# Row 0 of a fused attention and expert kernel: dilated transposes moved forward, dilated v cast by its load, the last product stored in two parts

## The chip, the cores and the metric

The kernel runs on one core of a Trainium2 chip. The metric is the device time of one execution in microseconds (us). Of the kernel before, five runs and one profiled execution are shown.

## What is computed

Attention over 8 batch rows, each with 8 heads, 576 positions and 64 numbers per head, then an expert layer over all 4608 tokens. Heads 0 to 3 look at the last 32 positions ("sliding"), heads 4 to 7 at every fourth of the last 128 ("dilated").

```
scores = q @ k.T / sqrt(64);  masked outside the window
attn   = exp(scores - max) / (sum + 1e-9)
x      = (attn @ v), heads side by side: 4608 x 512
out    = relu(x @ w_in)**2 @ w_out        # w_in 512 x 2048, w_out 2048 x 512, out float32
```

## The kernel before

The program is unrolled and written in order by hand: each engine carries out its instructions in the order in which the source issues them, and the framework adds the waits. What orders the work around the change is therefore the source order and the queues: SyncE's (SP) and GpSimd's (POOL) each issue their transfers one after the other, and a transfer that waits holds up those behind it.

Tokens go through the expert layer in nine chunks of 512 columns (`mm1_gen`: products with w_in, line 298, relu on ScalarE, line 321, square on VectorE, line 322; then products with w_out). Chunks 2 to 8 take the second product by one level of Strassen's scheme (`mm2_strassen_gen`): seven products of halves, in PSUM banks called a, b and c (matmuls in line 375), joined by copies on ScalarE (line 391) and sums on VectorE (line 402) in the SBUF tiles `ou` and `ov`, and stored by `leave` (line 397). Attention of row b is written between steps ("pump") of the expert chunk before it, so TensorE has expert matmuls while other engines do softmax.

Row 0 has no chunk before it. There TensorE is kept occupied by `fill_gen` (line 507): pairs of 128x512 matmuls whose result nobody reads, one pair for each pump. Row 0 goes as follows.

- GpSimd issues four loads that cast float32 to float16: `ns` (sliding k, then q, line 112) and `nd` (dilated k, then q, line 103). GpSimd then makes a position table and the identity matrix.
- VectorE clears tiles and makes the masks `maskp` and `maskd`. It writes into `sv` and `sd` a few values of `ns` (lines 759, 761), which holds back SyncE's loads of v into those tiles until `ns` is there.
- SyncE loads v in float32 into the staging tiles `sv` (six loads, line 129) and `sd` (two loads, line 137). GpSimd casts them into `vp` (line 169) and `vd` (line 177), with a fourth column block for the row sums; between these casts it issues the three parts of w_in (`wi`, line 146).
- TensorE transposes q and k (`t_sliding`, line 536; `t_dilated`, line 553); VectorE and ScalarE copy the results to `QKTp` and `QKTd` (lines 163, 165).
- Scores (`s_sliding`, line 573, twice; `s_dilated`, line 592, twice) go to PSUM tiles of a pool with two buffers; ScalarE takes the exponential (line 563), VectorE multiplies by the mask (line 564).
- ScalarE copies the overlap of neighbouring blocks inside `vp` and `vd` ("halo", lines 184, 189).
- Values (`av_sliding`, line 622, three times; `av_dilated`, line 638, four times) are divided by the row sums on VectorE (reciprocal, line 605, product, line 610), transposed on TensorE (lines 651, 669) and copied into `xT` on ScalarE (lines 657, 675). Then the first expert chunk starts.

The order of row 0 in the source before:

```
t_sliding x2; s_sliding 0; fill; s_sliding 1; fill; halo; t_dilated x2; halo; fill;
av_sliding 0; fill; s_dilated 0; fill; s_dilated 1; fill; halos; av_sliding 1 and 2; ...
```

The tile `sd` also serves later rows; its upper 64 partitions of the first part are cleared once at the start. The pool `gp`, with two buffers, holds the hidden values `g` of the expert chunks. [...]

Of the kernel before, what the change touches and what calls it, by code (L numbers as in the profile page):

```python
# [8 lines left out]
FP16 = mybir.dt.float16  # L9
# [4 lines left out]
P = 128  # L14
# [3 lines left out]
def kernel(  # L18
# [9 lines left out]
    nc = tc.nc  # L28

    B, H, S, D = q.shape  # L30
    W = 32
    DIL = 4
# [3 lines left out]
    HH = H // 2  # L36
# [62 lines left out]
    def load_qk(b):  # L99
        n = load_sliding_qk(b)  # L100
        m = natp.tile([P, 36 * D], FP16, name=f"nd{b}", tag="n")
        for i, s in ((1, k), (0, q)):
            nc.gpsimd.dma_start(
                out=m[64 * i : 64 * (i + 1), :],
                in_=s[b, HH:H].rearrange("h (p j) d -> (h p) (j d)", j=36),
            )
        return n, m
# [23 lines left out]
            for h in (0, 2):  # L131
                nc.sync.dma_start(out=sv[PADP:P, h : h + 2], in_=vv[:, h : h + 2])

    def load_dilated_v(b, eng):
        vv = v[b, HH:H].rearrange("h (i c) d -> i h (c d)", c=DIL)
        for t in range(2):
            eng.dma_start(out=sd[P - QD[t] : P, t, :, :], in_=vv[Q0D[t] : Q0D[t] + QD[t]])
# [2 lines left out]
        load_sliding_v(b)  # L140
        load_dilated_v(b, nc.sync)

    def load_w_in():
        f0 = 0
        for t, w in zip(wi, wi_cols):
            nc.gpsimd.dma_start(
                out=t, in_=moe_w_in[:, f0 : f0 + w].rearrange("(dh dl) f -> dl dh f", dl=P)
            )
            f0 += w

    def load_w_out(gs):
        for g in gs:
# [14 lines left out]
    def cast_sliding_v(b, ms=range(0, NB, 2)):  # L167
        for m in ms:
            nc.gpsimd.tensor_copy(  # L169
                vp[b % 2][:, m : m + 2, :, 0:D], sv[:, :, m : m + 2, :].rearrange("p h m d -> p m h d")  # L170
            )

    def cast_dilated_v(b):
        for t in range(2):
            p0 = 64 * t
            for c in range(0, DIL, 2):
                nc.gpsimd.tensor_copy(  # L177
                    vd[b % 2][p0:P, t, c : c + 2, :, 0:D],
                    sd[p0:P, t, :, D * c : D * (c + 2)].rearrange("p h (c d) -> p c h d", d=D),
                )  # L180

    def halo_sliding(b, mp):
        m0, m1 = max(1, 2 * mp), 2 * mp + 2
        nc.scalar.copy(
            vp[b % 2][0:PADP, m0:m1, :, 0:D], vp[b % 2][P - PADP : P, m0 - 1 : m1 - 1, :, 0:D]
        )
# [49 lines left out]


    nsd = {0: load_qk(0)}
    warm = const.tile([P, 1], FP32, name="warm")
    nc.vector.memset(warm, 0.0)  # L240
    nc.scalar.activation(warm, warm, ACTF.Exp)
    nc.vector.memset(sv[0:PADP, :, 0, :], 0.0)
    nc.vector.memset(sd[0:64, 0, :, :], 0.0)
    nc.vector.memset(sv[0:PADP, :, 1:NB, :], 0.0)
    for r in range(2):
        nc.vector.memset(QKTp[r][:, 1, :, 0:PADP], 0.0)
# [5 lines left out]
    reli = const.tile([P, QB], I16, name="reli")  # L252
    nc.gpsimd.iota(reli, pattern=[[1, QB]], base=0, channel_multiplier=-1)
    make_identity(nc, ident)

    relf = const.tile([P, QB], FP32, name="relf")
    nc.vector.tensor_copy(relf, reli)
# [95 lines left out]
    def mm2_strassen_gen(c, g):  # L353
        A, Bk, Ck = "abc"
        banks = {}

        def wq(r, q):
            return lambda k: wo[2 * r + k // 4][:, k % 4, HM * q : HM * (q + 1)]

        def gq(i, r):  # L360
            return lambda k, t: g[:, HF * r + k, HTOK * i + P * t : HTOK * i + P * (t + 1)]

        def tq(n):
            return lambda k: wt[n][:, k]

        def sq(n):
            return lambda k, t: gs[n][:, k, P * t : P * (t + 1)]

        def product(bank, a, b, ts=(0, 1)):
            new = bank not in banks  # L370
            if new:
                banks[bank] = pmool.tile([P, 2, HM], FP32, name=f"p{bank}{c}", tag="pm")
            for t in ts:
                for k in range(HF):
                    nc.tensor.matmul(  # L375
                        banks[bank][:, t],
                        a(k, t),
                        b(k),
                        start=(new and t == 0 and k == 0),
                        stop=(k == HF - 1),  # L380
                        skip_group_check=True,
                    )
                    if k % 4 == 3 and (t, k) != (ts[-1], HF - 1):
                        yield

        def half(i):
            return otp.tile([P, 2, DM], FP32, name=f"o{i}_{c}", tag="ot")

        def take(o, j):
            ot = o[:, :, HM * j : HM * (j + 1)]  # L390
            nc.scalar.copy(ot, banks[A])  # L391
            return ot

        def leave(o, i, js):
            t0 = c * TOKC + HTOK * i
            m = slice(HM * js[0], HM * (js[-1] + 1))
            nc.sync.dma_start(
                out=out[t0 : t0 + HTOK, m].rearrange("(t p) m -> p t m", p=P), in_=o[:, :, m]
            )

        def add(ot, bank):
            nc.vector.tensor_add(ot, banks[bank], ot)  # L402

        last = c == NTOKC - 1

        nc.vector.tensor_sub(g[:, 0:HF, HTOK:], g[:, 0:HF, 0:HTOK], g[:, 0:HF, HTOK:])
        yield from product(A, gq(0, 0), wq(0, 0))
        upper = half("u")
        o11 = take(upper, 0)
        yield  # L410
        yield from product(Ck, gq(0, 1), wq(1, 0), (0,))
        yield
        yield from product(A, sq(1), tq(1))
        lower = half("v")
        o21 = take(lower, 0)
        yield
        yield from product(Bk, gq(1, 0), tq(2))
        nc.vector.tensor_sub(gs[1], g[:, HF:, 0:HTOK], gs[1])
        yield
        yield from product(A, sq(0), tq(0))  # L420
        o22 = take(lower, 1)
        add(o22, Bk)
        if last:
            leave(lower, 1, (1,))
        yield
        yield from product(Ck, gq(0, 1), wq(1, 0), (1,))
        add(o11, Ck)
        if last:
            leave(upper, 0, (0,))
        yield  # L430
        yield from product(A, sq(1), wq(1, 1))
        take(upper, 1)
        leave(upper, 0, (1,) if last else (0, 1))
        yield
        yield from product(Bk, gq(1, 1), tq(3))
        add(o21, Bk)
        leave(lower, 1, (0,) if last else (0, 1))
        yield

    def mm2(c, g, po, t, ffc):  # L440
# [71 lines left out]
    def pump(n):  # L512
        for _ in range(n):
            while pending:
                try:
                    next(pending[0])
                    break
                except StopIteration:
                    pending.pop(0)
# [28 lines left out]
    def t_dilated(b, n, a, wide):  # L548
        for w, (s0, s1) in enumerate(((0, 5), (5, 9))):
            p_ = pt(f"pd{b}_{a}_{w}", wide)  # L550
            for s in range(s0, s1):
                j = 4 * s + 2 * a
                nc.tensor.transpose(  # L553
                    p_[:, P * (s - s0) : P * (s - s0 + 1)], n[:, D * j : D * (j + 2)], ident
                )
            copy(
                nc.scalar if w else nc.vector,
                QKTd[b % 2][:, :, a, KPAD:].rearrange("x i (c s) -> x i c s", s=9)[:, :, :, s0:s1],
                p_[:, 0 : P * (s1 - s0)].rearrange("x (s i c) -> x i c s", i=2, c=64),
            )  # L560
# [5 lines left out]
    def s_sliding(b, hp):  # L566
        tiles = [pa(f"ps{b}_{hp}_{half}") for half in range(2)]
        for half, ps in enumerate(tiles):
            for m3 in range(3):
                m = 3 * half + m3  # L570
                for e in range(2):
                    r = slice(D * e, D * (e + 1))
                    nc.tensor.matmul(  # L573
                        ps[:, e, QB * m3 : QB * (m3 + 1)],
                        QKTp[b % 2][r, 1, hp, QB * m : QB * m + P],
                        QKTp[b % 2][r, 0, hp, PADP + QB * m : PADP + QB * (m + 1)],
                        start=True,
                        stop=True,
                    )
        for half, ps in enumerate(tiles):  # L580
            softmax(2 * hp + half, ps, maskp)
# [176 lines left out]
    n, m = nsd[0]  # L758
    nc.vector.tensor_copy(sv[64:P, 0, :, 0], n[0:64, 0, 0:NB])
    load_sliding_v(0)  # L760
    nc.vector.tensor_copy(sd[64:P, :, 0, 0], n[0:64, 0, 0:2])
    load_dilated_v(0, nc.sync)
    cast_sliding_v(0, (0, 2))
    load_w_in()
    cast_sliding_v(0, (4,))
    cast_dilated_v(0)
    for hp in range(2):
        t_sliding(0, n, hp, False)
    pending.append(fill_gen())
    for hp in range(2):  # L770
        s_sliding(0, hp)
        pump(1)
    halo_sliding(0, 0)
    for a in range(2):
        t_dilated(0, m, a, False)
    halo_sliding(0, 1)
    pump(1)
    xs = x_tiles(0)
    av_sliding(0, 0, xs)
    pump(1)  # L780
    for g in range(2):
        s_dilated(0, g)
        pump(1)
    halo_sliding(0, 2)
    for c in (0, 2):
        halo_dilated(0, c)
# [146 lines left out]
```

## Time and profile before

| | us |
|---|---|
| median of 5 runs (lowest, highest) | 309.16 (307.81, 311.26) |
| profiled execution, its own time | 310.32 |
| its span | 308.5 |
| TensorE busy (share) | 288.2 (93%) |
| VectorE busy | 209.6 (68%) |
| ScalarE busy | 173.2 (56%) |
| GpSimd busy | 63.9 (21%) |
| first transposes of row 0 that have k and q, start | 6.87 |
| first run of back-to-back expert matmuls, start | 26.03 |
| last sum, start | 304.68 |
| last store, issue | 305.40 |

The span is what the profiler saw between first and last instruction; the execution's own time is 1.8 us longer. A line of the timeline has start, length, engine, source line, operation, tiles and shapes, how many instructions were merged into it, and in brackets the idle time before it with what ended that. PE is TensorE, DVE VectorE, ACT ScalarE, POOL GpSimd, SP SyncE; a q behind an engine's name is its queue. Lines of the chain have start, length, engine, tile and line.

### The profile page before, as it was taken

Reading aid. Unit: us, or ns where it says so; the run is one execution under the profiler, and the core shown is the slowest. Engines: PE = TensorE matmul, PEld = TensorE weight load, DVE = VectorE, ACT = ScalarE, POOL = GpSimd, SP = SyncE. Lnnn points to the kernel's source line nnn. Section 1 sums busy time; section 2 is a strip of 40 time slices with the busy share of each in tenths; the row PEclk is TensorE's granted clock in tenths of the full one; section 3 lists DMA queues with packets and bytes.
Section 4 is the critical chain, followed back from the end, with each engine's and each line's share of the span. In section 5 each row is a group of like instructions: output and inputs, shape, how many; then the busy total and the mean of one; then the engine's idle time right before and its main releaser. Section 6 shows DMA issues by size and latency. Waiting matters only on the chain.

```text
span 308.5 us, 6899 instructions
## 1 busy us (share of the span) xinstructions
PE 288.2 (93%) x2762; PEld 193.7 (63%) x2762; DVE 209.6 (68%) x434; ACT 173.2 (56%) x293; POOL 63.9 (21%) x112
## 2 busy tenths in 40 slices
PE   1988998999999899999997999899989999999994
PEld 1544554555554468756886997458745875685584
DVE  7785447758942698489758993889388934834652
ACT  2765648668745863495356634854495436525620
POOL 4480027002803602410026002700230000000000
PEclk9999999999999999999999999999999999999999
DMA  7899999699599999995799979989891141003004
GB/s 121 190 208 211 208 158 155 150 201 234 121 214 149 253 186 187 249 205 119 124 180 265 192 128 185 277 177 140 159 255 39 23 103 52 2 1 136 2 1 137
DMA packets 77616, 47.03 MB, mean 152 GB/s; under 512 B 58480, under 2 KB 69232, under 8 KB 77584
## 3 DMA queue, kind: packets, MB, share of 16 engines
q1 hardware_dynamic: 68832, 32.96, 51.0%
q0 software_dynamic: 8752, 13.63, 25.6%
q8 instruction: 21, 0.34, 0.5%
q14 instruction: 11, 0.09, 0.1%
HBM read 36.70 MB, written 16.52 MB: 172 GB/s over the span
## 4 chain that ended last, share of the span: by engine, by line
PE 81%; DMA 9%; DVE 4%; ACT 3%; issue 1%; SPq 0%; POOL 0%; DVEq 0%; POOLq 0%
PE ph L298 33%; PE pa L375 16%; PE po L441 9%; PE pb L375 8%; DMA vp<-vp 6%; PE pc L375 4%; PE paw L638 3%; PE pav L622 2%; DMA QKTp<-dp 2%; PE ps L573 2%; DMA ns<-in_q_dram 2%; ACT AT L563 2%; PE pf L507 2%; DVE AT L564 1%; PE pd L553 1%
## 5 line engine op out<-in xcount | busy, mean ns | idle before, releaser
L298 PE MATMUL ph<-xT,wi 128*128 128x512 f16 (+1 forms) x640 | 134.2, 359 | 0.7 <-ACT xT L675 0.7
L321 ACT ACTIVATE rt<-ph 128x512 f16<-128x512 f32 x144 | 86.2, 609 | 48.4 <-PE ph L298 46.2
L298 PEld LDWEIGHTS <-wi 128*128 128x128 f16 x640 | 68.2, 114 | 45.9 <-issue 0.6
L322 DVE TENSOR_TENSOR g<-rt 128x512 f16<-128x512 f16 x144 | 62.5, 444 | 40.1 <-ACT rt L321 38.7
L375 PEld LDWEIGHTS <-g 128*128 128x128 f16 x448 | 43.3, 98 | 6.1
L375 PEld LDWEIGHTS <-gs 128*128 128x128 f16 x336 | 32.1, 98 | 3.9 <-DVE gs L332 0.3
L441 PE MATMUL po<-wo,g 128*128 128x512 f16 x128 | 33.1, 379 | 0.0
L402 DVE TENSOR_TENSOR ov<-pb,ov 128x512 f32<-128x512 f32 x14 | 9.7, 692 | 30.9 <-PE pb L375 17.4
L375 PE MATMUL pa<-wt,gs 128*128 128x256 f16 x224 | 27.2, 273 | 0.0
L375 PE MATMUL pb<-wt,g 128*128 128x256 f16 x224 | 27.1, 273 | 0.0
L169 POOL CAST vp<-sv 128x512 f16<-128x512 f32 x24 | 15.4, 671 | 55.7 <-DMA sv<-in_v_dram 51.7
L391 ACT COPY ov<-pa 128x512 f32<-128x512 f32 x14 | 8.2, 585 | 30.7 <-PE pa L375 30.7
L177 POOL CAST vd<-sd 128x512 f16<-128x512 f32 (+1 forms) x32 | 21.9, 712 | 10.7 <-PE ph L298 7.9
L610 DVE TENSOR_TENSOR xd<-paw,rcp_d 80x512 f16<-80x512 f32 (+1 forms) x32 | 21.9, 685 | 1.1
L563 ACT ACTIVATE AT<-pz 128x576 f16<-128x576 f32 x32 | 19.7, 696 | 1.5 <-PE pz L592 1.4
L563 ACT ACTIVATE AT<-ps 128x576 f16<-128x576 f32 x32 | 19.2, 658 | 2.5 <-PE ps L573 2.0
L564 DVE TENSOR_TENSOR AT<-AT,maskp 128x576 f16<-128x576 f16 x32 | 15.6, 496 | 6.3 <-ACT AT L563 4.6
L564 DVE TENSOR_TENSOR AT<-AT,maskd 128x576 f16<-128x576 f16 x32 | 18.5, 604 | 1.8 <-ACT AT L563 0.6
L391 ACT COPY ou<-pa 128x512 f32<-128x512 f32 x14 | 8.2, 586 | 16.3 <-PE pa L375 16.3
L610 DVE TENSOR_TENSOR xs<-pav,rcp_p 96x512 f16<-96x512 f32 x24 | 16.5, 686 | 0.8
L622 PEld LDWEIGHTS <-AT 128*128 128x128 f16 x192 | 9.5, 99 | 11.9 <-issue 7.3
L622 PE MATMUL pav<-vp,AT 128*128 128x65 f16 x192 | 10.9, 196 | 5.6 <-DMA vp<-vp 4.5
(80 smaller groups left out, 279.3 us busy)
## 6 DMA issues: line engine op xcount, KB each, us to landing
sv<-in_v_dram SPq DMA_DIRECT2D x14, 288.0 KB, 5.3
dp<-nr SPq DMA_DIRECT2D x12, 288.0 KB, 4.1
out_dram<-ou SPq DMA_DIRECT2D x6, 512.0 KB, 4.2
out_dram<-ov SPq DMA_DIRECT2D x6, 512.0 KB, 4.6
sd<-in_v_dram SPq DMA_DIRECT2D x8, 320.0 KB, 6.4
ns<-in_k_dram POOLq DMA_DIRECT2D x8, 288.0 KB, 6.2
ns<-in_q_dram POOLq DMA_DIRECT2D x8, 288.0 KB, 7.9
sd<-in_v_dram SPq DMA_DIRECT2D x8, 256.0 KB, 6.2
```

What stands on the lines that cost most here:

```text
L169: nc.gpsimd.tensor_copy(vp[b % 2][:, m : m + 2, :, 0:D], sv[:, :, m : m + 2, :].rearrange("p h m d -> p m h d"))
L177: nc.gpsimd.tensor_copy(vd[b % 2][p0:P, t, c : c + 2, :, 0:D], sd[p0:P, t, :, D * c : D * (c + 2)].rearrange("p h (c d) -> p c h d", d=D),)
L298: nc.tensor.matmul(ph[:, t0:t1], wi4[ffc // 4][:, dmk, :, ffc % 4], xT[:, dmk, x0 : x0 + t1 - t0], start=(dmk == 0 and t0 == 0), stop=(dmk ...
L321: nc.scalar.activation(rt, ph[:], ACTF.Relu)
L322: nc.vector.tensor_mul(g[:, ffc, :], rt, rt)
L375: nc.tensor.matmul(banks[bank][:, t], a(k, t), b(k), start=(new and t == 0 and k == 0), stop=(k == HF - 1), skip_group_check=True,)
L391: nc.scalar.copy(ot, banks[A])
L441: nc.tensor.matmul(po, g[:, ffc, t * P : (t + 1) * P], wo[ffc // 4][:, ffc % 4, :], start=(ffc == 0), stop=(ffc == NFF - 1),)
L563: nc.scalar.activation(AT[:, u, 0:UW], ps[:, :, 0 : UW // 2], ACTF.Exp, scale=scale)
L564: nc.vector.tensor_mul(AT[:, u, 0:UW], AT[:, u, 0:UW], mask)
L610: nc.vector.tensor_tensor(out=x, in0=pv, in1=rb, op=ALU.mult)
L622: nc.tensor.matmul(pav[:, i, h * (D + 2) : h * (D + 2) + D + 1], AT[:, 2 * (h // 2) + m // 3, off : off + P], vp[b % 2][:, m, h, 0 : D + 1 ...
```

## The change

The float32 staging of row 0's dilated v is left out. A float16 tile `sd16`, taken from the pool of the hidden values, is loaded instead, by GpSimd's queue, which casts on the way; the two loads stand behind the identity matrix and ahead of the first cast of sliding v. VectorE clears the part of `sd16` that the loads don't write, and ScalarE copies that zero to `sd` for the later rows. Four copies on VectorE, between the two halves of the dilated scores, place `sd16` into `vd`, where GpSimd had four casts. The parts of w_in are issued between the casts of sliding v: the first part behind the first cast, the others behind the second.

On TensorE the dilated transposes go ahead of the second sliding scores, the dilated scores ahead of the first sliding values, and there is one fill pair less. The halo copies are spread accordingly.

At the end of the last chunk the last product and its sum are written in two parts of 128 tokens, each with a store of its own.

```diff
@@ -131,7 +131,7 @@
             for h in (0, 2):
                 nc.sync.dma_start(out=sv[PADP:P, h : h + 2], in_=vv[:, h : h + 2])
 
-    def load_dilated_v(b, eng):
+    def load_dilated_v(b, eng, sd=sd):
         vv = v[b, HH:H].rearrange("h (i c) d -> i h (c d)", c=DIL)
         for t in range(2):
             eng.dma_start(out=sd[P - QD[t] : P, t, :, :], in_=vv[Q0D[t] : Q0D[t] + QD[t]])
@@ -140,13 +140,12 @@
         load_sliding_v(b)
         load_dilated_v(b, nc.sync)
 
-    def load_w_in():
-        f0 = 0
-        for t, w in zip(wi, wi_cols):
+    def load_w_in(ns):
+        for n in ns:
+            t, w, f0 = wi[n], wi_cols[n], sum(wi_cols[:n])
             nc.gpsimd.dma_start(
                 out=t, in_=moe_w_in[:, f0 : f0 + w].rearrange("(dh dl) f -> dl dh f", dl=P)
             )
-            f0 += w
 
     def load_w_out(gs):
         for g in gs:
@@ -236,11 +235,16 @@
 
 
     nsd = {0: load_qk(0)}
+    sd16 = gp.tile([P, NFF, TOKC], FP16, name="sd16", tag="g")
+    sd16 = sd16[:, 0:4].rearrange("p a w -> p (a w)").rearrange(
+        "p (t h x) -> p t h x", t=2, h=HH
+    )
     warm = const.tile([P, 1], FP32, name="warm")
     nc.vector.memset(warm, 0.0)
     nc.scalar.activation(warm, warm, ACTF.Exp)
     nc.vector.memset(sv[0:PADP, :, 0, :], 0.0)
-    nc.vector.memset(sd[0:64, 0, :, :], 0.0)
+    nc.vector.memset(sd16[0:64, 0], 0.0)
+    nc.scalar.copy(sd[0:64, 0], sd16[0:64, 0])
     nc.vector.memset(sv[0:PADP, :, 1:NB, :], 0.0)
     for r in range(2):
         nc.vector.memset(QKTp[r][:, 1, :, 0:PADP], 0.0)
@@ -252,6 +256,7 @@
     reli = const.tile([P, QB], I16, name="reli")
     nc.gpsimd.iota(reli, pattern=[[1, QB]], base=0, channel_multiplier=-1)
     make_identity(nc, ident)
+    load_dilated_v(0, nc.gpsimd, sd16)
 
     relf = const.tile([P, QB], FP32, name="relf")
     nc.vector.tensor_copy(relf, reli)
@@ -432,9 +437,17 @@
         take(upper, 1)
         leave(upper, 0, (1,) if last else (0, 1))
         yield
-        yield from product(Bk, gq(1, 1), tq(3))
-        add(o21, Bk)
-        leave(lower, 1, (0,) if last else (0, 1))
+        if last:
+            for t in range(2):
+                yield from product(Bk, gq(1, 1), tq(3), (t,))
+                o = o21[:, t]
+                nc.vector.tensor_add(o, banks[Bk][:, t], o)
+                t0 = c * TOKC + HTOK + P * t
+                nc.sync.dma_start(out=out[t0 : t0 + P, 0:HM], in_=o)
+        else:
+            yield from product(Bk, gq(1, 1), tq(3))
+            add(o21, Bk)
+            leave(lower, 1, (0, 1))
         yield
 
     def mm2(c, g, po, t, ffc):
@@ -758,29 +771,35 @@
     n, m = nsd[0]
     nc.vector.tensor_copy(sv[64:P, 0, :, 0], n[0:64, 0, 0:NB])
     load_sliding_v(0)
-    nc.vector.tensor_copy(sd[64:P, :, 0, 0], n[0:64, 0, 0:2])
-    load_dilated_v(0, nc.sync)
-    cast_sliding_v(0, (0, 2))
-    load_w_in()
+    cast_sliding_v(0, (0,))
+    load_w_in((0,))
+    cast_sliding_v(0, (2,))
+    load_w_in((1, 2))
     cast_sliding_v(0, (4,))
-    cast_dilated_v(0)
     for hp in range(2):
         t_sliding(0, n, hp, False)
     pending.append(fill_gen())
-    for hp in range(2):
-        s_sliding(0, hp)
-        pump(1)
-    halo_sliding(0, 0)
+    s_sliding(0, 0)
     for a in range(2):
         t_dilated(0, m, a, False)
+    pump(1)
+    s_sliding(0, 1)
+    pump(1)
+    xs = x_tiles(0)
+    s_dilated(0, 0)
+    halo_sliding(0, 0)
+    pump(1)
+    for t in range(2):
+        for c in range(0, DIL, 2):
+            nc.vector.tensor_copy(
+                vd[0][64 * t : P, t, c : c + 2, :, 0:D],
+                sd16[64 * t : P, t, :, D * c : D * (c + 2)].rearrange("p h (c d) -> p c h d", d=D),
+            )
+    s_dilated(0, 1)
     halo_sliding(0, 1)
     pump(1)
-    xs = x_tiles(0)
     av_sliding(0, 0, xs)
     pump(1)
-    for g in range(2):
-        s_dilated(0, g)
-        pump(1)
     halo_sliding(0, 2)
     for c in (0, 2):
         halo_dilated(0, c)
```

## The prediction

> **What bounds the kernel now.** I read the page first, for busy shares and the chain; then the chain in order of time; then the timeline of the first 27 us and of the last 6; then single tiles (nd, sv, pb) for landings and durations.
>
> From the page:
>
> ```profile
> PE 288.2 (93%) x2762; PEld 193.7 (63%) x2762; DVE 209.6 (68%) x434; ACT 173.2 (56%) x293; POOL 63.9 (21%) x112
> ```
>
> TensorE is busy for 288.2 of 308.5 us. Some 7 of its 20 idle microseconds lie before the first transpose, 4 after its last matmul; whatever comes between 26 and 304 us is TensorE's own work, which the change leaves alone. So only two places can pay: when full-rate expert matmuls start, and the end. The chain in order of time (start, length, what):
>
> ```profile
> 2.04 4.78 DMA ns<-in_q_dram
> 11.57 1.92 PE pd L553 x18
> ...
> 23.49 0.68 DVE xd L610
> 24.32 0.69 DVE xd L610
> 25.39 0.59 ACT xT L675
> 26.03 13.11 PE ph L298 x60
> ...
> 302.90 1.76 PE pb L375 x16
> 304.68 0.69 DVE ov L402
> ```
>
> Row 0 ends in a VectorE chain (xd), a ScalarE copy, then 60 matmuls back to back from 26.03. The second list is the end: product, sum, store. The timeline of the head shows what fills VectorE (start, length, engine, line, idle time before):
>
> ```profile
> 11.09 1.23 DVE L564 TENSOR_TENSOR AT<-AT,maskp 128x576 f16<-128x576 f16 x2 [0.57 <-ACT AT L563]
> ...
> 15.53 2.61 ACT L563 ACTIVATE AT<-pz 128x576 f16<-128x576 f32 x4 [0.81 <-PE pz L592]
> ...
> 16.21 0.46 DVE L564 TENSOR_TENSOR AT<-AT,maskd 128x576 f16<-128x576 f16 x1 [0.44 <-ACT AT L563]
> ...
> 16.68 2.96 POOL L177 CAST vd<-sd 128x512 f16<-128x512 f32 x4 [0.79 <-DVE AT L564]
> ...
> 16.86 2.31 DVE L564 TENSOR_TENSOR AT<-AT,maskd 128x576 f16<-128x576 f16 x3 [0.19 <-ACT AT L563]
> ```
>
> One mask product takes 0.46 us alone and 0.74, 0.75 and 0.86 while GpSimd casts vd beside it. The last begins at 18.31 and ends at 19.17. From 19.09 to 25.00 VectorE does six pairs of reciprocal and product (0.84 us each, 0.66 of waits), and TensorE waits for them.
>
> **The change, part by part.**
>
> *The dilated transposes move ahead.* They go from behind two sets of sliding scores and two fill pairs to behind the first set. They need both nd loads. The q load is issued at 3.19 and takes 6.9 us (tile nd, narrow window), so it is there at 10.1; the first sliding scores end at 9.04. So TensorE now waits 1.06 us at the head of its queue; queued behind are transposes, second sliding scores and everything else of row 0. Transposes 10.10 to 12.02 (the 1.92 of the chain). A fill pair at the early rate (0.97) to 13.0. Second sliding scores; their first exponential starts 0.46 after (8.38 to 8.84 now), at 13.5, against 10.41 before. ScalarE gets two exponentials (1.19) to 14.7. TensorE does its second fill pair until 14.6 and then dilated scores, whose exponential follows 0.35 later (15.18 to 15.53 now), at 14.95 instead of 15.53. Four exponentials when fed take 2.28 (row 1, 50.00), and the first vp halo copy, 0.40, now lies between them: end at 17.6 instead of 18.14. What is won is the end of work that stood around the scores, 0.5 us; what is lost is that the sliding scores are three microseconds late, which nothing needs before the sliding values.
>
> *GpSimd no longer casts vd.* Its four casts (2.96 us) go. VectorE's last mask product follows the last exponential by 0.46 plus some 0.1 for the queue: 18.15 to 18.2, not 19.17. That is 1.0 us, half from the earlier exponentials and half from products that run alone.
>
> *VectorE places vd.* Four f16 copies of 512 elements between second and third dilated mask product, waiting for the new load; behind them stand those products and all sums of row 0. No row shows this copy. The nearest, the f16 SBUF copy nr (128x2304, 0.74), gives 0.16 by elements; with the 0.10 to 0.17 of the smallest VectorE rows 0.28. The other end is a copy out of PSUM, QKTp (576 elements, 0.71): 0.63. I take 0.28, since types, memory and runs of 64 elements are those of nr. VectorE starts one instruction some 0.08 before the last ends (18.31 plus 0.86 is 19.17, the next starts at 19.09), so the four take 0.9. They fit where VectorE would wait for the third exponential, from 16.5 to 17.4; without that cover they would cost 0.9.
>
> *The first sliding values move back.* Before, their reciprocal and product stood at 14.85 to 15.78, in a wait. Now they stand behind the last mask product: seven pairs, not six, so 0.84 more on the path. 1.0 minus 0.84 is 0.15 to 0.2 won. One fill pair less (0.43 at the later rate) lies in TensorE's waits: nothing. **Head: minus 0.2.**
>
> *Loads.* Two vd loads leave SyncE's queue (issues at 11.05, 1.75 us); SyncE's next is the sv load at 27.33, so nothing. They enter GpSimd's at 4.58, 0.6 us each by the nd issues, inside its 6.46 us of waiting for sv; if that cover were gone the first sliding cast and w_in would be 1.2 later, and w_in has slack (landed 19.5 for a first use at 22.48). The landings of k and q (5.4, 6.8, 8.65, 10.1) are 1.45 apart for 288 KB, so 288 KB more behind nd land at 11.6 alone, and by 14 if sv has half the engines; needed at 16.5. The sliding loads share for that time and may come 1 us later; their halos have 2 us. The first w_in part leaves 1.3 us earlier, w_out some 4 us; nothing waits for either in the trace. In the built order GpSimd then waits for the first two w_in parts to land before it issues the last nd half and wo2; used after 44, so nothing. Zeroing through ScalarE (64x1024, 1.1 us by the 0.64 of 576) lies in its 5.37 us of idleness; were it late, the vd load would wait.
>
> *The end.* VectorE may add the first half once eight products are done; but in the changed kernel's order the ninth matmul waits for VectorE. Last of the first eight starts at 303.51 and is out 0.27 later; add of 256 columns 0.44 (0.69 for 512, 0.19 for 8, linear); with two hand-overs of 0.03 the ninth starts at 304.29 instead of 303.62: plus 0.67. Second add 0.44 instead of 0.69: minus 0.25. The last store is half as big:
>
> ```profile
> 306.50:306.75 0.25, 0.00 (x0) 0.00 (x0) 0.00 (x0) 0.00 (x0) 0.00 (x0) 1.00 1.01 348
> ```
>
> At these 348 GB/s (last column) 128 KB less is minus 0.37 of the 2.2 us to landing. Bounds: no saving in the landing, plus 0.42; no stall, minus 0.62. **End: plus 0.05.**
>
> [...]
>
> Sum: the profiled execution took 310.32 us (span 308.5), 1.16 above the median of 309.16. Minus 0.2 plus 0.05 gives 310.2 for it, and 309.0 against the median.
>
> **The clock of TensorE.** Fill pairs are 1.01 us at 13.36 and 0.63 at 14.62, at a granted clock of 1.00 in both rows. I assume the faster rate from the same time on. Now 1.06 us of waiting and one fill pair less stand before it.
>
> ```profile
> 13.36 1.01 PE L507 MATMUL pf<-maskp,ident 128*128 128x512 f16 x2
> 14.62 0.63 PE L507 MATMUL pf<-maskp,ident 128*128 128x512 f16 x2
> ```
>
> If it came 3 us later, scores and values up to 17.7 would run at about half rate; most of that lies under ScalarE and VectorE, and 0.3 would show, 1.0 at worst (two fill pairs at 0.54 more).
> [...]
>
> **Rivals.**
> 1. *VectorE becomes the bound (slower).* If the copies run like QKTp's, four take 4 x 0.63 less overlap, 2.3 instead of 0.9, before the third mask product. Plus 1.4: mm1 from 27.2, 310.4. It decides from 0.33 us a copy, where the head's gain is gone. For it: nothing shows such a copy; against it: nr's row.
> 2. *Casts were the real load (faster).* If TensorE's reciprocal hand-overs tighten too, that is, the 0.66 of waits between the six pairs goes and copies take 0.16, the head wins 1.2; with the end's better bound, 307.4 to 308.
> [...]
> 4. *Split end does not do what it says.* All stall and no shorter landing: plus 0.42, 309.4.
>
> **How the numbers follow.** Forecast, within half a microsecond of 309.0: 0.5; rival 1: 0.17; rival 2: 0.15; rivals 3 and 4: 0.18. Worst bounds together: 1.4 plus 1.0 plus 0.4, 311.9; best: 307.4. I leave out the corner and add a little for runs that spread 3.4 us: 307.0 to 311.3. 1% is 3.1 us, about what a measurement of this kernel tells from no change. No sum above reaches it; surprises downstream, in DMA order above all, are the rest: faster by more 0.11, within 0.76, slower 0.13.
>
> **What would show it.** Right: first pd transpose near 10.1; copies near 0.28; dilated mask products at 0.46; last one ended near 18.2; 60 matmuls from 25.8; a gap of 0.67 in the last sixteen; a landing of 1.8. Wrong: copies above 0.4, transposes after 11, fill pairs of 1 us past 15, or w_in awaited by TensorE; and a shift of over 2 us that arises after 27 us.

## The result, and the profile after

The changed kernel takes 312.03 us (median; 309.7 to 316.91) against 309.15 (306.76 to 314.27) for the kernel before: a ratio of 1.0091, 95% interval [1.0074, 1.0108]. I had forecast 309.0, range 307.0 to 311.3. It is slower by 0.9% and lies outside the range. Ratios here and below leave out slow executions (those over 1.5% above the fastest of their kernel), medians hold them; the traces of e1 and e6 are of slow ones.

The one profiled execution doesn't show that at first sight. Its own time is 310.42 us and its span 308.6, beside 310.32 and 308.5 before. TensorE's busy time has hardly moved (287.5 us after, 288.2 before), so the 60 matmuls of the first expert chunk, the landmark of the prediction, come first. From the page (busy time, share and instructions of each engine), and from the chain of the changed kernel in order of time (start, length, what):

```profile
PE 287.5 (93%) x2760; PEld 193.0 (63%) x2760; DVE 210.7 (68%) x438; ACT 173.7 (56%) x294; POOL 61.9 (20%) x110
```
```profile
3.16 7.43 DMA nd<-in_q_dram
10.73 2.08 PE pd L566 x18
...
15.64 1.19 ACT AT L576 x2
...
25.61 0.70 DVE xd L623
26.68 0.59 ACT xT L688
27.32 13.11 PE ph L303 x60
```

They start at 27.32, not 26.03: the head of row 0 costs 1.29 us more, where I had 0.2 less. Why the span doesn't show it is in the chain of waits, TensorE's part, from the first expert matmuls to the last product (us in total, times, longest). Before, then after:

```profile
PE pav L622 <- DMA vp<-vp: 4.5, 3, 2.1
PE ps L573 <- DMA QKTp<-dp: 1.5, 1, 1.5
```
```profile
PE pav L635 <- DMA vp<-vp: 3.6, 3, 1.7
PE ps L586 <- DMA QKTp<-dp: 0.8, 1, 0.8
```

These are waits of later rows for halo copies and transposes by DMA. They came to 6.0 us in the traced execution of before and 4.4 in that of after, 1.6 less, which hid the head's loss. It isn't only luck: the other traces with before's head have 5.0 to 5.5 (e0_before_again, e1, e7), those with the changed head 4.5 and 3.5 (e0_after_again, e5). Whether the later head shortens these waits was not tested.

The timeline of the head (start, length, engine, line, operation, count, idle time before) shows where the head loses:

```profile
13.54 0.61 POOL L168 CAST vp<-sv 128x512 f16<-128x512 f32 x1 [7.72 <-DMA sv<-in_v_dram]
...
14.76 1.24 DVE L577 TENSOR_TENSOR AT<-AT,maskp 128x576 f16<-128x576 f16 x2 [1.51 <-ACT AT L576]
...
16.32 1.00 DVE L577 TENSOR_TENSOR AT<-AT,maskd 128x576 f16<-128x576 f16 x2 [0.33 <-ACT AT L576]
...
17.11 0.68 POOL L168 CAST vp<-sv 128x512 f16<-128x512 f32 x1
...
17.17 1.16 ACT L576 ACTIVATE AT<-pz 128x576 f16<-128x576 f32 x2
17.24 1.43 DVE L794 COPY vd<-sd 128x512 f16<-128x512 f16 x4
...
18.70 0.83 DVE L577 TENSOR_TENSOR AT<-AT,maskd 128x576 f16<-128x576 f16 x2
...
19.44 0.20 DVE L618 RECIPROCAL rcp_p<-pav 96x8 f32<-96x8 f32 x1
```

From 16.32 VectorE has no pause over 0.1 us until the sums. ScalarE does the last two dilated exponentials from 17.17 in 1.16, so the third is ready near 17.8, half a microsecond after the copies began, and its mask product starts only at 18.70. The last mask product ends at 19.53; I had 18.15 to 18.2. And GpSimd's first sliding cast is at 13.54, 2.5 us later than the 11.04 of before.

The end, the same view:

```profile
302.85 1.04 PE L380 MATMUL pb<-wt,g 128*128 128x256 f16 x8
...
303.93 0.42 DVE L444 TENSOR_TENSOR ov<-pb,ov 128x256 f32<-128x256 f32 x1 [1.59 <-PE pb L380]
304.38 1.90 SPq L446 DMA_DIRECT2D out_dram<-ov  x2
304.40 1.03 PE L380 MATMUL pb<-wt,g 128*128 128x256 f16 x8 [0.52 <-DVE ov L444]
...
305.47 0.42 DVE L444 TENSOR_TENSOR ov<-pb,ov 128x256 f32<-128x256 f32 x1 [1.12 <-PE pb L380]
```

The second eight matmuls wait 0.52 us for the first sum, as forecast (0.67). The last store is issued at 305.9 (the two issues end at 306.28) and lands 1.7 us later. From the first matmul of the product to that landing it is 4.8 us; before, 302.74 to 305.40 plus 2.2, it is 4.9. The split end changes next to nothing.

### The profile page after: what moved, and what is told of

It reads as the page before. It is cut to its first block, busy times and chain, and to the rows that moved or that the text cites. A ratio compares the mean times of both kernels' runs of the same rounds, so it can differ in the third digit from the quotient of the medians.

```text
span 308.6 us, 6897 instructions
## 1 busy us (share of the span) xinstructions
PE 287.5 (93%) x2760; PEld 193.0 (63%) x2760; DVE 210.7 (68%) x438; ACT 173.7 (56%) x294; POOL 61.9 (20%) x110
## 4 chain that ended last, share of the span: by engine, by line
PE 74%; DMA 14%; DVE 5%; ACT 4%; issue 1%; POOL 1%; SPq 0%; DVEq 0%; POOLq 0%
PE ph L303 31%; PE pa L380 15%; PE po L454 7%; PE pb L380 7%; DMA vp<-vp 6%; PE pc L380 4%; PE paw L651 3%; DMA nd<-in_q_dram 2%; ACT AT L576 2%; DMA QKTp<-dp 2%; PE pav L635 2%; DMA ns<-in_q_dram 2%; DVE AT L577 2%; DMA QKTd<-dd 1%; DVE g L327 1%
## 5 line engine op out<-in xcount | busy, mean ns | idle before, releaser
L327 DVE TENSOR_TENSOR g<-rt 128x512 f16<-128x512 f16 x144 | 63.6, 452 | 39.7 <-ACT rt L326 38.5
L407 DVE TENSOR_TENSOR ov<-pb,ov 128x512 f32<-128x512 f32 x13 | 9.0, 692 | 28.4 <-PE pb L380 14.9
L380 PE MATMUL pb<-wt,g 128*128 128x256 f16 x224 | 27.2, 273 | 0.5 <-DVE ov L444 0.5
L380 PE MATMUL pa<-wt,gs 128*128 128x256 f16 x224 | 27.2, 273 | 0.0
L168 POOL CAST vp<-sv 128x512 f16<-128x512 f32 x24 | 14.7, 645 | 53.7 <-DMA sv<-in_v_dram 36.6
L176 POOL CAST vd<-sd 128x512 f16<-128x512 f32 (+1 forms) x28 | 19.6, 726 | 10.9 <-PE ph L303 9.3
L396 ACT COPY ou<-pa 128x512 f32<-128x512 f32 x14 | 8.2, 585 | 16.5 <-PE pa L380 16.5
L623 DVE TENSOR_TENSOR xs<-pav,rcp_p 96x512 f16<-96x512 f32 x24 | 16.5, 686 | 0.8
```

The costliest lines, as they stand in the source:

```text
L168: nc.gpsimd.tensor_copy(vp[b % 2][:, m : m + 2, :, 0:D], sv[:, :, m : m + 2, :].rearrange("p h m d -> p m h d"))
L176: nc.gpsimd.tensor_copy(vd[b % 2][p0:P, t, c : c + 2, :, 0:D], sd[p0:P, t, :, D * c : D * (c + 2)].rearrange("p h (c d) -> p c h d", d=D),)
L327: nc.vector.tensor_mul(g[:, ffc, :], rt, rt)
L380: nc.tensor.matmul(banks[bank][:, t], a(k, t), b(k), start=(new and t == 0 and k == 0), stop=(k == HF - 1), skip_group_check=True,)
L623: nc.vector.tensor_tensor(out=x, in0=pv, in1=rb, op=ALU.mult)
```

## The experiments

My theory after this had two parts: (A) the dilated v loads, queued first by GpSimd, hold SyncE's sliding loads back; (B) the new order on TensorE pushes work into a stretch in which VectorE is full, and the four copies lie in it too. The rival for both was that the traced head is one unlucky draw of DMA and clock, and that the loss lies downstream or at the end. Source lines shift by up to some 10 between them. The table has the start of the 60 expert matmuls in each kernel's trace, and its ratio to the kernel before, measured beside it.

| kernel | 60 matmuls from | median us | ratio [95%] |
|---|---|---|---|
| e0_before_again | 25.48 | 310.07 | 0.9950 [0.9905, 0.9995] |
| e1: before, split end | 26.41 | 309.79 | 1.0022 [0.9992, 1.0053] |
| e7: before, split end in two banks | 25.69 | 309.85 | 0.9978 [0.9938, 1.0018] |
| e0_after_again | 27.32 | 311.65 | 1.0079 [1.0043, 1.0114] |
| e5: after, whole end | 27.21 | 312.85 | 1.0072 [1.0033, 1.0112] |
| e2: before, new order only | 27.03 | 310.49 | 1.0034 [1.0004, 1.0064] |
| e3: before, new v path only | 27.56 | 313.24 | 1.0090 [1.0048, 1.0132] |
| e4: after, v loads later | 26.77 | 310.44 | 1.0035 [1.0004, 1.0067] |
| e6: e3, v loads later | 26.11 | 314.15 | 1.0053 [1.0004, 1.0102] |
| e8: before, float32 v loads ahead | 30.01 | 315.02 | 1.0211 [1.0166, 1.0257] |
| e9: after, copies earlier | 26.07 | 311.83 | 1.0041 [1.0002, 1.0080] |
| e10: e9, two banks | 26.38 | 312.41 | 1.0100 [1.0055, 1.0145] |

**How large is noise? The two controls.** The kernel before, unchanged:

> The kernel before once more, as a control and for a second trace of it. Ratio 1.000, interval holding 1. If its trace again shows TensorE waiting 1.5 us near 100 us for the transposed q and k of row 3, that wait belongs to the kernel; if not, it belongs to the execution.

An identical kernel came out at 0.995 with an interval that just leaves out 1: 0.5%, or 1.5 us, is what such a comparison can be off. Its trace does show the wait near 100 us again (1.7 us), so by the test stated above it belongs to this kernel; the changed head's traces have 0.8 there or none (e1 and e7, 0.8 and 0.7 in several waits). Its expert matmuls start at 25.48. The four traces with before's head (before, e0, e1, e7) start at 25.48 to 26.41, mean 25.90.

The changed kernel, unchanged:

> The changed kernel once more, as a control and for a second trace. If its one trace was typical, 60 matmuls start at 27.0 to 27.5 and the ratio is 1.007 to 1.011. Theory A (the dilated v loads, queued first on GpSimd's queue, hold SyncE's sliding loads back): sliding casts again at 13 to 14, 14.5 to 15.5 and 16.5 to 17.5, where before has 11.0, 12.4 and 15.2, and sliding v landings of 5 us and more. Rival (that trace caught an unlucky execution): casts near 11 and 12.5, matmuls from 26.2 or earlier.

Matmuls again from 27.32, first sliding cast at 13.70. With e5 the three traces of the changed head give 27.21 to 27.32, mean 27.28. The head's loss is thus 1.4 us (27.28 less 25.90), 0.8 to 1.8 from the extremes, and not bad luck. The spans of the two second traces are 307.0 and 308.8: there the head's 1.84 is the whole difference.

**The end.** Before with only the new end, and after with only the old end:

```diff
+ if last:                       # e1; e5 takes the same lines out of after
+     for t in range(2):
+         product half t; add half t; store half t
- yield from product(Bk, gq(1, 1), tq(3)); add(o21, Bk); leave(lower, 1, (0,))
```

> The kernel before, with only the last product, sum and store in two parts. All theories agree on the place: a gap of about 0.5 us on TensorE between the first and the last eight matmuls of the last product, and the last sum as late. Theory 'the end pays nothing': the shorter sum (0.42 for 0.69) and a landing 0.3 to 0.4 shorter give it back, ratio 1.000. Theory 'the end costs': landing as long as before, 0.3 to 0.5 us more, ratio 1.001 to 1.0016. Head as before: 60 matmuls from 26.0.

> The changed kernel with last product, sum and store whole again. If the split end costs 0.5 us of the loss and the rest is the head: ratio 1.006 to 1.008, last sum 0.69, no gap among the last sixteen matmuls, expert matmuls from 27 to 27.6. If the end's gap is given back by the shorter landing: ratio as the changed kernel, 1.009.

e1 is not told from 1, and e5 stays as slow as the changed kernel. The loss isn't in the end.

The changed end leaves a wait of 0.52 us, with both halves in the tile of bank b. e7 gives each half of the last product, and of the one before it that uses bank b, its own PSUM bank:

```diff
- product((t,)) into Bk, sum from banks[Bk][:, t]
+ product((t,)) into (Bk, Dk)[t], sum from banks[(Bk, Dk)[t]][:, t]
```

> The kernel before with its last product, sum and store in two parts, each part in a PSUM bank of its own. If the gap at the end comes from both parts lying in one bank: no gap among the last sixteen matmuls, last sum 0.42 right behind them, its landing 1.7 to 1.8, end 0.5 to 0.7 us sooner than before, ratio 0.998. If the gap comes from something else (the sum's queue, the store): a gap of 0.5 as in the split alone, ratio 1.001.

The timeline of the end of e7:

```profile
301.74 1.04 PE L375 MATMUL pb<-wt,g 128*128 128x256 f16 x8
302.61 1.04 PE L375 MATMUL pd<-wt,g 128*128 128x256 f16 x8
302.81 0.42 DVE L448 TENSOR_TENSOR ov<-pb,ov 128x256 f32<-128x256 f32 x1 [1.52 <-PE pb L375]
303.26 1.22 SPq L450 DMA_DIRECT2D out_dram<-ov  x2
303.69 0.42 DVE L448 TENSOR_TENSOR ov<-pd,ov 128x256 f32<-128x256 f32 x1 [0.45 <-PE pd L375]
```

The second eight follow the first without a gap, and the first sum lies beside them. The second store is issued at 304.1 (the issues end at 304.48) and lands 1.7 later: 4.1 us from the first matmul to the landing, 0.8 less than the 4.9 of before. My better bound had been 0.62. In whole times it can't be seen: 0.9978 with an interval that holds 1.

**The place of the loads.** First the new v path alone, in before's order; then the same with the two loads issued behind the first sliding cast; and the changed kernel with them there:

```diff
  make_identity(nc, ident)
- load_dilated_v(0, nc.gpsimd, sd16)     # e3 keeps it here
...
  cast_sliding_v(0, (0,))
+ load_dilated_v(0, nc.gpsimd, sd16)     # e6 (order of before) and e4 (order of after)
```

> The kernel before, with only the new way of dilated v (cast in the load on GpSimd's queue ahead of the sliding casts, four VectorE copies between the halves of the dilated scores, w_in issued between the sliding casts); order on TensorE and end as before. Theory A: sliding loads land 2 us later or more, first sliding cast at 13.5 instead of 11.0, w_in from 14 instead of 13.0; here the first sliding values stand ahead of the dilated scores, so TensorE waits 1 to 2 us there and expert matmuls run from 27.0 to 28.5, ratio 1.005 to 1.010. Theory B: nothing waits for sliding v, VectorE is freed of GpSimd's company, from 25.2 to 25.8, ratio 0.997 to 0.999.

> Order on TensorE and end of the kernel before; dilated v by the cast in GpSimd's load, but issued behind the first sliding cast, and placed by four VectorE copies between the halves of the dilated scores. Theory A (the place in the queue hurts, the way itself does not): first sliding cast at 11.0, mask products of 0.46 beside no GpSimd cast, four copies in 1.2, last mask product ended by 19.0, expert matmuls from 25.5 to 26.0, ratio 0.998 to 1.000. Theory B' (the way itself hurts, VectorE pays for the copies what GpSimd did before): last mask product ended after 19.5, from 26.3 or later, ratio 1.002 or more.

> The changed kernel, with the two loads of dilated v behind the first cast of sliding v instead of ahead of it; order on TensorE, copies and split end stay. Theory A: nd at 10.1, sliding v cast at 11.0 and 12.5, dilated v there by 15, mask products as in the changed kernel, expert matmuls from 25.7 to 26.0, time within 0.5 us of before (ratio 1.000 to 1.002, the split end included). Theory B: from 27.0 or later, ratio 1.006 or more, as the changed kernel.

In e3 TensorE stands still for 3.20 us, because ScalarE's copies of QKTd are queued behind the halo copy, and that waits for the late cast of sliding v (at 13.46). The timeline of e3, TensorE:

```profile
15.17 0.59 PE L512 MATMUL pf<-maskp,ident 128*128 128x512 f16 x2 [3.20 <-ACT QKTd L162]
```

With the loads later (e6) the cast is back at 11.52, the stall is 0.65 and the expert matmuls start at 26.11 instead of 27.56: 1.45 us. Not all of that need be the queue: behind the stall of e3 fill pairs take 1.04 us (17.39 and 18.95) after 0.59 at 15.85, and in e6 they take 0.59 to 0.61 from 13.35 on. In the changed kernel's order (e4) the same move is worth 0.5 (26.77 against 27.28, between what my two theories said); there the sliding values are wanted later. By ratios it would be 1.4 to 1.7 us (1.0035 against 1.0079 and 1.0091). Casts, copies and mask products in the timeline of e4:

```profile
11.05 0.61 POOL L168 CAST vp<-sv 128x512 f16<-128x512 f32 x1 [6.50 <-DMA sv<-in_v_dram]
...
16.97 1.15 DVE L794 COPY vd<-sd 128x512 f16<-128x512 f16 x4
...
18.16 0.83 DVE L576 TENSOR_TENSOR AT<-AT,maskd 128x576 f16<-128x576 f16 x2
```

The same of e6:

```profile
11.52 0.73 POOL L168 CAST vp<-sv 128x512 f16<-128x512 f32 x1 [6.97 <-DMA sv<-in_v_dram]
...
17.29 1.11 DVE L791 COPY vd<-sd 128x512 f16<-128x512 f16 x4
```

e6 shows the gain of the new path alone, free of the queue: none (26.11 against 25.90). GpSimd's casts are gone, but the copies take 1.11 us of VectorE. Its ratio of 1.0053 and median of 314.15 aren't explained by its head: its trace has two long waits for DMA halos in later rows (2.48 and 2.53 us), and a mean granted clock of 0.987, against 1.000 in the trace of before. That the change made either likelier was not shown.

Is it the place in the queue, or the casting on the way? e8 is the kernel before with the float32 loads at the changed kernel's place, uncast:

```diff
  make_identity(nc, ident)
+ load_dilated_v(0, nc.gpsimd)
...
- load_dilated_v(0, nc.sync)
```

> The kernel before, with only one thing moved: the float32 loads of dilated v are issued by GpSimd, behind the identity matrix, where the changed kernel issues its casting loads; casts on GpSimd, order on TensorE and end as before. Theory A (place in the queue): SyncE's sliding loads are held back as in the changed kernel or more, since 576 KB and not 288 KB are written; first sliding cast at 13 or later, 60 matmuls 1 to 1.6 us later than before's 26.03, ratio 1.004 to 1.009. Rival (it is the casting on the way that is slow, not the place): first sliding cast at 11.0 to 11.7 and matmuls from 25.8 to 26.3, ratio 0.998 to 1.002.

The timeline of e8:

```profile
14.99 0.61 POOL L169 CAST vp<-sv 128x512 f16<-128x512 f32 x1 [9.10 <-DMA sv<-in_v_dram]
...
16.69 1.01 PE L508 MATMUL pf<-maskp,ident 128*128 128x512 f16 x2 [3.38 <-ACT QKTd L163]
```

The place. The first cast is 4 us late, TensorE stalls 3.38, and the matmuls start at 30.01, far beyond my 1 to 1.6: with 576 KB instead of 288 ahead of them, the sliding loads took some 7.0 us each. Of the 4.0 us, 3.3 are there when the stall ends (16.69, against 13.36 for the same fill pair before); the rest arises while TensorE is slow (fill pairs of 1.01 to 1.04 until 20.6, of 0.63 from 14.62 on before). The queues of the changed kernel and of before say the same. The DMA view, window 9 to 11 us (packets, MB, share of 16 engines, where overlapping packets can add up to over 100%; q0 is GpSimd's queue, q1 SyncE's). Before:

```profile
q1 hardware_dynamic: 1290, 0.32, 71.1%
q0 software_dynamic: 13, 0.02, 5.2%
```

After:

```profile
q0 software_dynamic: 563, 0.31, 114.6%
q1 hardware_dynamic: 209, 0.05, 12.6%
```

SyncE's loads were issued from 7.01 on in the changed kernel, earlier than before (7.3). Yet in this window they move 0.05 MB instead of 0.32, while GpSimd's queue moves 0.31; from 11 to 13, with GpSimd's loads all but done (0.03 MB), they move 0.42.

**The order on TensorE.** The kernel before with only the order of the changed one (loads, casts and end as before):

```diff
- s_sliding 0, s_sliding 1, t_dilated x2, av_sliding 0, s_dilated 0, s_dilated 1
+ s_sliding 0, t_dilated x2, s_sliding 1, s_dilated 0, s_dilated 1, av_sliding 0
```

> The kernel before, with only the order on TensorE (and what follows it on ScalarE and VectorE) of the changed kernel; dilated v still comes by SyncE in float32 and is cast on GpSimd. Theory A (the new load of dilated v on GpSimd's queue is what hurts): nd there at 10.1, sliding v cast from 11.0, expert matmuls back to back from 25.8 to 26.3, ratio 0.999 to 1.001. Theory B (the order itself hurts, by the wait for nd and by the sliding values put last): from 27.0 or later, ratio 1.004 to 1.008.

27.03, so the order alone costs 1.1 against the mean of 25.90, 0.6 against the latest of before's heads; in this execution the first loads were 0.5 to 0.8 late. Short fill pairs came late too (0.68 us at 15.88, against 0.63 at 14.62 in before), and this one trace doesn't separate that. The first sliding cast was early (11.67, not 13.5), so here it isn't the loads. VectorE's sums began at 19.17, at the same time as before's 19.09, though the four mask products still ran beside the casts; but seven pairs of reciprocal and product follow, to 26.01, not six.

**What in that stretch binds?** If VectorE does, then work taken out of it is won whatever the loads do. e9 puts the four copies ahead of the second sliding scores, into VectorE's 1.51 us of waiting:

```diff
  t_dilated x2; fill
+ for t ...: nc.vector.tensor_copy(vd[0]..., sd16...)     # four copies
  s_sliding(0, 1); fill; s_dilated(0, 0); ...
- for t ...: nc.vector.tensor_copy(vd[0]..., sd16...)
  s_dilated(0, 1)
```

> The changed kernel with VectorE's four copies of dilated v ahead of the second sliding scores instead of between the dilated ones. Theory B (VectorE is the bound of row 0 from its first late mask product on, so what is taken out of that stretch is won): copies at 13.3 to 14.6 in VectorE's wait, last dilated mask product ended near 18.8 instead of 19.53, 60 matmuls from 26.5 to 26.8 instead of 27.32. Rival (the late sliding casts bind): mask products end earlier but the sums wait for vp, and matmuls still start at 27.2 to 27.4. Second rival: the load lands later than 13.3 and VectorE's mask products queue behind the copies, matmuls from 27.5 on.

The timeline of e9:

```profile
12.93 1.35 DVE L788 COPY vd<-sd 128x512 f16<-128x512 f16 x4
13.32 0.61 POOL L168 CAST vp<-sv 128x512 f16<-128x512 f32 x1 [7.49 <-DVE vd L788]
...
15.90 2.38 DVE L577 TENSOR_TENSOR AT<-AT,maskd 128x576 f16<-128x576 f16 x4
...
26.07 8.14 PE L303 MATMUL ph<-xT,wi 128*128 128x512 f16 x37 [0.67 <-ACT xT L688]
```

The sliding cast is as late as in the changed kernel (13.32), and still the last mask product ends at 18.28, not 19.53, and the matmuls start at 26.07. e10, with the same head, starts them at 26.38. Against 27.28 that is 0.9 to 1.2 us for moving four copies. Part of it could be TensorE's rate. In the traces of e9, e10, e5 and both of the changed kernel fill pairs take 1.00 to 1.04 us up to a point and 0.59 to 0.62 behind it, at a granted clock of 1.00 in every window from 12 to 18 us; what sets that point was not shown. The first short pair starts at 13.75 in e9, at 14.02 in e10, and at 15.54 and 15.77 in the two traces of the changed kernel. e5 speaks against that: same head as the changed kernel, first short pair at 14.11, and no gain. The same view of e5:

```profile
14.11 0.60 PE L512 MATMUL pf<-maskp,ident 128*128 128x512 f16 x2
...
15.11 1.20 ACT L568 ACTIVATE AT<-pz 128x576 f16<-128x576 f32 x2
...
16.65 1.16 ACT L568 ACTIVATE AT<-pz 128x576 f16<-128x576 f32 x2
...
17.14 1.42 DVE L786 COPY vd<-sd 128x512 f16<-128x512 f16 x4
...
18.60 0.83 DVE L569 TENSOR_TENSOR AT<-AT,maskd 128x576 f16<-128x576 f16 x2
...
27.21 7.07 PE L303 MATMUL ph<-xT,wi 128*128 128x512 f16 x32 [0.67 <-ACT xT L680]
```

There the dilated exponentials start at 15.11, nearly as I had forecast (14.95), and the copies in the middle take back what that won. In e10 ScalarE is at the same place:

```profile
16.61 1.17 ACT L585 ACTIVATE AT<-pz 128x576 f16<-128x576 f32 x2
...
16.63 1.96 DVE L586 TENSOR_TENSOR AT<-AT,maskd 128x576 f16<-128x576 f16 x4
```

The exponentials end at 17.8 in both. The last mask product ends at 18.59 in e10 and at 19.43 in e5, and the matmuls start at 26.38 and 27.21: with ScalarE's work alike, and fill pairs of 0.60 us from 14.02 and 14.11 on, the place of the copies is worth 0.8 us.

Last, e9's head with e7's end, meant as the best form of the change:

> The changed kernel with the copies ahead of the second sliding scores, and at the end a PSUM bank for each half of the last two products and sums. If both theories hold: matmuls from 26.5 to 26.8 and from the first matmul of the last product to the landing 4.1 us instead of 4.77, so 1.3 to 1.5 us less than the changed kernel and 0.1 us less to 0.1 more than before: ratio to before 0.998 to 1.003, to the changed kernel 0.994 to 0.997. If only the end holds: 0.7 less than the changed kernel, ratio 1.004 to 1.008.

The head (26.38) is 0.1 better than expected, and the end as expected if the store lands 1.7 after its issue as in e7 (first matmul 305.61, issue at 308.0: 4.1); but the time isn't: 312.41, ratio 1.0100. In its trace TensorE waits 5.2 us for halos by DMA in later rows, and after the longest, 2.7 us up to 169.5, its granted clock falls to 0.55 (windows: stretch, length, busy PE, PEld, DVE, ACT, POOL, granted clock, DMA share, GB/s):

```profile
171.10:174.40 3.30, 3.30 (x29) 2.49 (x28) 2.29 (x6) 1.20 (x2) 0.00 (x0) 0.55 0.74 143
174.50:178.00 3.50, 3.50 (x48) 3.48 (x45) 2.80 (x7) 1.84 (x4) 0.00 (x0) 1.00 0.80 180
```

No run shows that these waits come from head or end, so e10 stays a miss without a settled cause (its ratio rests on six executions). No kernel here is shown to beat the one before.

**What adds up.** Comparing only executions with the granted clock at 0.9985 or more throughout, the median span is 309.0 us for the changed kernel (27 executions) and 307.1 for the one before (43, from the comparisons with e1, e5 and e0_after_again and from e0_before_again). The 1.9 between them is near the head's 1.4. The medians of whole times differ by 2.9 in the first measurement and 1.8 beside e0_after_again. So the head's part is shown, and 0.4 to 1.5 us more is not located; the control says that a comparison can be off by that much. Lost clock isn't more frequent in the changed kernel: 27 of its 56 executions pass this bar, 43 of 103 of the one before.

## Why the prediction was wrong

*The step that failed: "They fit where VectorE would wait for the third exponential, from 16.5 to 17.4; without that cover they would cost 0.9."* Only half of the cover was there. VectorE reached the copies at 17.24, the third exponential was ready near 17.8, and the copies took 1.43, to 18.67. The fourth exponential ended at 18.33; without the copies the last mask product (0.46) would have ended near 18.8, my estimate from these rows, and not at 19.53. So they cost some 0.7, where I had put nothing. In e5 VectorE reached them at 17.14 for an exponential ready near 17.3: almost no cover. e9 and e10, with the copies where VectorE does wait, get 0.9 to 1.2 back. I had computed when ScalarE would be late, but not when VectorE would arrive: its sliding mask products had moved behind the waiting for nd, to 14.76. My own rows didn't give the cover either: exponentials from 14.95 (1.19 for two), the halo copy (0.40) and one exponential more end at 17.1, not 17.4. Rival 1 had the place (copies ahead of the third mask product) and nearly the size (matmuls from 27.2; they start at 27.32), but for a wrong reason, a slow copy; that its size fits is luck. The copy was as I had it.

*Size of a copy: right.* The tile view of the changed kernel (minimum, median, maximum in ns):

```profile
L794 DVE COPY vd<-sd x4: 281/290/699, 17.2 to 18.4; 128x512 f16<-128x512 f16 x2, 64x512 f16<-64x512 f16 x2
```

0.28 to 0.29, as taken from nr; the 0.70 is the first, which began beside GpSimd's late third sliding cast (17.11 to 17.79) and ended 0.15 us after it. In e4, where that cast was over at 16.35 and the copies began at 16.97, the largest of the four took 0.39. So this may be one way in which the late loads reach VectorE, some 0.3 us; that the cast made the copy longer was not shown by itself.

*"The sliding loads share for that time and may come 1 us later": mis-sized.* The first cast came 2.5 us later (13.54 for 11.04). I had given each queue half of the engines; from 9 to 11 us GpSimd's queue had nearly all of them (114.6% against 12.6%). In packets it was 563 against 209. In the new order this costs 0.5 us by the start of the matmuls (e4, one trace), of which the longer first copy (0.70 us, at most 0.39 in e4) may be part. It also turns round my "first w_in part leaves 1.3 us earlier": it left at 14.10, 1.1 later than before's 12.98, though no matmul of the chunk is seen waiting for it. My landings of k and q were 1.4, 1.8 and 1.5 apart, not evenly 1.45; dilated v was there at 12.8 all the same, well ahead of its copies.

*nd there at 10.1: 0.6 short.* Transposes began at 10.73; the q load took 7.4 us, not 6.9. In the other traces of this order they began at 10.29 to 10.85. This delayed everything behind it by 0.2 to 0.75, and I had allowed nothing. It is the other half of the late mask products: the exponentials ended at 18.33 where I had 17.6. The change isn't needed to explain it: in e0_before_again the same load also took 7.4. I had put the landing of one execution on the path.

*GpSimd's casts gone: right in the main.* All four dilated mask products took 0.45 to 0.46 in the profiled execution; in e0_after_again one took 0.75, with no cast from 15.85 to 17.29, and in e5 one took 0.87, where the late third sliding cast (16.77 to 17.68) may have taken the place of the missing ones. *Seventh pair: right.* Seven take 19.44 to 26.29, 6.85 us, against 5.91 for six: 0.94 for my 0.84. Together with e2 this says that the order's price was mostly known; what was missing was the price of the copies and of the late inputs. In sum: the last mask product came 1.35 later than forecast and the seventh pair cost 0.1 more, which turns my minus 0.2 for the head into plus 1.29.

*A later clock: seems off the path.* The first short fill pair (0.62 us after, 0.63 before) starts 1.15 us later in the profiled pair (15.77 against 14.62), but e5, with it at 14.11, starts its matmuls only 0.1 earlier (27.21 against 27.32). The 0.3 to 1.0 that I had put on a later clock, and with it the 1.0 in the sum of worst bounds, was my estimate, and no run shows it: the granted clock was 1.00 from 12 to 18 us in all three, and the runs show that 0.1 in its place.

*End: right.* About minus 0.1 for my plus 0.05. With both halves in one bank TensorE waited 0.52 us for the first sum (in e1 too), with two banks (e7) it didn't wait. The second bank is a second tile too, and no run separates the two.

*The range* failed only in part with the first step. The head's 1.4 alone would give 309.16 plus 1.4, or 310.6, still inside; the median lies above 311.3, and even above the 311.9 of all worst bounds, only with the part that is not located. Still, my three costs were bounded one by one (VectorE 1.4, clock 1.0, end 0.4), and I had left out the corner, although late inputs, a full VectorE and a first copy of 0.70 us came together here.

## What to carry to other kernels

Cover for a moved instruction is worked out on both sides: when the thing that it hides behind is late, and when the engine itself arrives with all that was moved ahead of it; if the engine comes late, what is left uncovered is on the path. A load queued early isn't free for the other queues: price it by the bytes ahead of the load that is wanted first (here the first sliding cast came 2.5 us later behind 288 KB and 4.0 behind 576). And two traces with equal spans don't say that nothing changed: read the landmark behind the change, and take a second trace of both kernels. A time of one execution, such as a landing, can move in the next (the q load took 6.9 and 7.4 us in two of one kernel); give it bounds.

## What I had not expected of the hardware

- Two loads, together 288 KB written, ahead on GpSimd's queue, held SyncE's loads of 96 KB to 5.4 to 6.1 us each, against 2.9 to 4.5 before; at 576 KB (e8) it was 6.8 to 7.4.
- Behind a wait of 2.7 us in e10 TensorE's granted clock was 0.55 from 171.10 to 174.40, so this wait may have cost more than its length. In the trace of before, with a wait of 2.1, the mean granted clock was 1.000. What tells the two apart was not shown.
- Two executions of one and the same program differed by 0.55 us in when row 0 ends (25.48 and 26.03 for the kernel before), as much as some of the edits studied here.
